# Threshold attention followed by hash routing on one core: routing in small pieces, scatters into two tables, and a leaner start

## The chip, the cores and the metric

The kernel runs on one core of one Trainium2 chip. The metric is device time in microseconds of one execution, as the median of several runs. A core has a matrix engine (TensorE, "PE" in the profile, with its weight loads shown as "PEld"), a vector engine (VectorE, "DVE"), an activation engine (ScalarE, "ACT"), a general engine (GpSimd, "POOL") and a queue engine (SyncE, "SP") that mainly issues DMA transfers. Every engine works through its own list of instructions in order and waits at semaphores for the others. In the profile "POOLq" and "SPq" are the instruction queues of these engines, where DMA transfers are issued.

## What is computed

The reference, cut to what matters:

```python
# attention: q, k, v are (8, 8, 576, 64), float32
scores = 0.125 * q @ k^T
thresh = max(scores, axis=-1) - tau
scores = where(scores >= thresh, scores, -1e9)
attn   = exp(scores - max(scores)); attn = attn / (sum(attn) + 1e-9)
out    = attn @ v
# bridge: (B, H, S, D) -> x of shape (4608, 512)
# routing: one of 8 experts per token, by its id
expert = token_ids * 2654435761 % 8
for e in range(8):
    xe = x[expert == e]
    out[expert == e] = relu(xe @ w1[e]) @ w2[e]     # w1 (8,512,1024), w2 (8,1024,512)
```

The routing depends on the token ids alone. It can therefore be worked out at any time before the first tokens are gathered for the first expert.

## The kernel before

The attention goes over 32 pairs of heads, `p` = 0 to 31, each in five steps `s` = 0 to 4 (`n = 5 p + s`): first the last 64 queries of both heads together, then four times 128 queries of each head. In each step PE computes scores, DVE turns them into `ns` (the negated scores, with their minimum accumulated), ACT takes the exponential, POOL computes the threshold `thr`, DVE masks and sums, PE transposes the weights, ACT copies them out of PSUM, and PE multiplies by v. POOL also scales the keys once per pair (`scale_k`) and adds an epsilon to the sums (`rec`). The instruction order of all engines is fixed by the program's order ("manual schedule").

The routing ranks each token within its expert, turns the rank into a slot, and writes the token's number to that slot of a table in DRAM by 36 indirect DMA transfers ("scatters") of 128 tokens each. The table is then loaded as `gidx`, by which the tokens are gathered for the experts from pair 26 on.

The loads of a pair, and the start of the kernel:

```python
def load_pair(p):
    ...
    for r in range(2):
        half = slice(64 * r, 64 * r + 64)
        nc.sync.dma_start(out=k_sb[half, 0], in_=kT[b, h0, :, S2 * r:S2 * r + S2])
        c0 = 64 * (1 - r)
        nc.sync.dma_start(out=k_sb[half, 1, c0:S2], in_=kT[b, h0 + 1, :, ...])
    nc.sync.dma_start(out=k_sb[0:64, 1, 0:64], in_=kT[b, h0 + 1, :, TAIL:S])
    for r in range(2):
        nc.sync.dma_start(out=q_sb[64 * r:64 * r + 64],
                          in_=qT[b, h0:h0 + 2].rearrange("h d s -> d h s"))

# first instructions
nc.sync.dma_start(out=tau_in[:], ...)
nc.sync.dma_start(out=tid32[:], ...)          # token ids
load_pair(0); load_v(0); load_pair(1)
make_identity(nc, ident[:])
...                                            # POOL: iotas, triangular matrix, ones, tables' fill
nc.sync.dma_start(out=slot_dram..., in_=none[:])
for w in w_bufs:                               # four buffers of 128 x 1152
    nc.vector.memset(w[:], 0.0)
...
nc.vector.memset(xg_bufs[0][:], 0.0)
for xg in xg_bufs[1:]:                         # nine copies
    nc.scalar.copy(xg[:], xg_bufs[0][:])
nc.vector.tensor_copy(iota_f[:], iota_i[:])
nc.vector.tensor_scalar(out=keep_any[:], in0=tau_in[:], ...)   # used by scale_k
```

The routing is a generator, `route()`, whose `yield` marks where a piece ends. One piece is issued ahead of the first score, and one in each step after that:

```python
def route():
    ...                                        # POOL: three memsets
    # piece 1: expert of each token, one-hot, scan along the tokens, counts by two matmuls
    nc.vector.tensor_scalar(out=eid[:], ...); nc.vector.tensor_copy(eidf[:], eid[:])
    nc.vector.tensor_tensor(out=onehot[:], ...)
    nc.vector.tensor_tensor_scan(incl[:]..., keep[:]..., onehot[:]..., ...)
    nc.vector.tensor_copy(row[:], incl[:, :, NTC - 1])
    nc.tensor.matmul(tr[:, 0, 0:E], lhsT=u128[:], rhs=row[:], start=True, stop=True)
    nc.tensor.matmul(tr[:, 0, E:2 * E], lhsT=ones128[:], rhs=row[:], start=True, stop=True)
    nc.vector.tensor_copy(cnt[:], tr[:, 0, 0:2 * E])
    ...
    yield
    ...                                        # pieces 2 to 4: base, rank, slot_i
    for c in range(NTC):                       # 36 scatters, one in each step
        yield
        ...                                    # in c = 1, 2, 3: overflow table on DVE
        nc.gpsimd.indirect_dma_start(
            out=slot_dram[:, :],
            out_offset=bass.IndirectOffsetOnAxis(ap=slot_i[:, c:c + 1], axis=0),
            in_=tok[:, c:c + 1], in_offset=None, ...)
    for _ in range(3):
        yield
    nc.sync.dma_start(out=gidx[0:TM], in_=slot_dram[0:E * CAP]...)
```

The main loop, cut to the order of what matters:

```python
for _ in range(24):
    nc.tensor.transpose(tr[:, 0, 0:P], ident[:], ident[:])    # PE works on nothing of use
next(pieces)
scale_k(0)
score(0, 0)
for n in range(LAST + NS + 1):
    p, s = divmod(n, NS)
    m = n - 2
    if s == 0: load_pair(p + 2); load_v(p + 1)
    if s == 1: scale_k(p + 1)                  # POOL
    q = p - 1
    if s == 1: add_eps(q)                      # POOL: rec
    if s == 2: nc.vector.reciprocal(recs[q][:], recs[q][:])
    ...
    negate(n, 0); expo(n, 0)                   # DVE ns, POOL thr; ACT
    if s == 0: put_xm(p - 2)                   # DVE xm, after ACT's xt
    ...
    score(n + 1, 0); negate(n, 1); expo(n, 1); score(n + 1, 1)
    ...
    for j in range(heads(n - 1)): mask(n - 1, j)               # DVE
    next(pieces, None)                         # a piece of the routing
    ...
```

Of the kernel before, what the change touches and what calls it, by code (L numbers as in the profile page):

```python
# [12 lines left out]
I32 = mybir.dt.int32  # L13
AF = mybir.ActivationFunctionType
ALU = mybir.AluOpType
AX = mybir.AxisListType
# [4 lines left out]
def kernel(  # L21
# [12 lines left out]
    nc = tc.nc  # L34

    B, H, D, S = qT.shape
    N, DIN = out.shape
    E, _, F = w1.shape
    P = 128
# [4 lines left out]
    NTC = N // P  # L44
    SCALE = 1.0 / float(D) ** 0.5
    assert D == 64 and S == 4 * P + 64 and SCALE == 0.125 and E == 8
    S2 = S // 2
    NQ = 4
    TAIL = NQ * P
# [6 lines left out]
    KT, TM = 5, 122  # L56
    CAP = KT * TM
    CH = CAP // 2
    NOV = 32
    NSLOT = -(-(E * CAP + NOV * P) // P) * P  # L60
    BIG = 1 << 20
# [4 lines left out]
    slot_dram = nc.dram_tensor("slot_scratch", (NSLOT, 1), I32, kind="Internal").ap()  # L66
# [21 lines left out]
    gidx = consts.tile([P, E, KT], I32, name="gidx")  # L88
    ov_i = consts.tile([P, NOV + 1], I32, name="ov_i")
# [28 lines left out]
    with tc.tile_pool(name="a_q", bufs=1) as a_q, \  # L118
# [29 lines left out]
        def load_pair(p):  # L148
            hp, b = divmod(p, B)
            h0 = 2 * hp  # L150
            q_sb = q_bufs[p % 3]
            k_sb = a_k.tile([P, 2, S2], FP32, name="k_sb")
            kts[p] = k_sb
            for r in range(2):
                half = slice(64 * r, 64 * r + 64)
                nc.sync.dma_start(out=k_sb[half, 0], in_=kT[b, h0, :, S2 * r:S2 * r + S2])
                c0 = 64 * (1 - r)
                nc.sync.dma_start(out=k_sb[half, 1, c0:S2],
                                  in_=kT[b, h0 + 1, :, (S2 - 64) * r:(S2 - 64) * r + S2 - c0])
            nc.sync.dma_start(out=k_sb[0:64, 1, 0:64], in_=kT[b, h0 + 1, :, TAIL:S])  # L160
            for r in range(2):
                nc.sync.dma_start(out=q_sb[64 * r:64 * r + 64],
                                  in_=qT[b, h0:h0 + 2].rearrange("h d s -> d h s"))
# [11 lines left out]
        def scale_k(p):  # L175
            nc.gpsimd.tensor_scalar(out=kts[p][:], in0=kts[p][:], scalar1=keep_any[:],
                                    scalar2=SCALE, op0=ALU.mult, op1=ALU.mult)
# [39 lines left out]
        def expo(n, j):  # L217
            c0 = 64 if n % NS == 0 else S * j
            w = w_bufs[n % NW][:, c0:c0 + S]
            ws[n, j] = w  # L220
            nc.scalar.activation(w, nss[n, j][:], AF.Exp, bias=stats[n][0][:, j:j + 1],  # L221
                                 scale=-1.0)
# [107 lines left out]
        def route():  # L330
# [24 lines left out]
            nc.gpsimd.memset(ones_e[:], 1.0)  # L355

# [4 lines left out]
            nc.vector.tensor_copy(eidf[:], eid[:])  # L361
            nc.vector.tensor_tensor(out=onehot[:],
# [3 lines left out]
            nc.vector.tensor_tensor_scan(incl[:].rearrange("p e c -> p (e c)"),  # L366
                                         keep[:].rearrange("p e c -> p (e c)"),
                                         onehot[:].rearrange("p e c -> p (e c)"),
                                         0.0, op0=ALU.mult, op1=ALU.add)
# [7 lines left out]
            nc.vector.tensor_copy(cnt[:], tr[:, 0, 0:2 * E])  # L377

# [4 lines left out]
                                    op0=ALU.logical_shift_right)  # L383
            nc.vector.tensor_copy(ot[:], ot_i[:])
            nc.vector.tensor_tensor_scan(oend[:], ones_e[:], ot[:], 0.0, op0=ALU.mult,
                                         op1=ALU.add)
            yield


            nc.vector.tensor_tensor(out=base[:], in0=oend[:], in1=ot[:], op=ALU.subtract)  # L390
            nc.vector.scalar_tensor_tensor(out=base[:], in0=base[:], scalar=8192.0,
                                           in1=cnt[:, 0:E], op0=ALU.mult, op1=ALU.add)
            nc.vector.tensor_tensor(out=incl[:], in0=incl[:],
                                    in1=base[:, :, None].to_broadcast([P, E, NTC]), op=ALU.add)
            nc.vector.tensor_tensor(out=incl[:], in0=incl[:], in1=onehot[:], op=ALU.mult)
            nc.vector.reduce_sum(rank_f[:], incl[:].rearrange("p e c -> p c e"), axis=AX.X)
            yield
            nc.vector.tensor_copy(rank_i[:, 0], rank_f[:])
            nc.vector.tensor_scalar(out=rank_i[:, 1], in0=rank_i[:, 0], scalar1=8191,
                                    scalar2=None, op0=ALU.bitwise_and)  # L400
            nc.vector.tensor_scalar(out=rank_i[:, 2], in0=rank_i[:, 0], scalar1=13, scalar2=None,
                                    op0=ALU.logical_shift_right)
            nc.vector.tensor_copy(rank[:], rank_i[:, 1])
            nc.vector.tensor_copy(ovt[:], rank_i[:, 2])
            yield
            nc.vector.tensor_scalar(out=first[:], in0=eidf[:], scalar1=float(CAP), scalar2=None,
                                    op0=ALU.mult)
            nc.vector.tensor_scalar(out=ovt[:], in0=ovt[:], scalar1=float(P),
                                    scalar2=float((E - 1) * CAP), op0=ALU.mult, op1=ALU.add)
            nc.vector.tensor_tensor(out=ovt[:], in0=ovt[:], in1=first[:], op=ALU.subtract)  # L410
            nc.vector.scalar_tensor_tensor(out=ovt[:], in0=rank[:], scalar=float(CAP),
                                           in1=ovt[:], op0=ALU.is_gt, op1=ALU.mult)
            nc.vector.tensor_tensor(out=first[:], in0=first[:], in1=rank[:], op=ALU.add)
            nc.vector.scalar_tensor_tensor(out=slot_i[:], in0=first[:], scalar=-1.0, in1=ovt[:],
                                           op0=ALU.add, op1=ALU.add)
            for c in range(NTC):
                yield
                if c == 1:
                    nc.vector.tensor_tensor(
                        out=oc[:], in0=iota_f[:, 0:NOV, None].to_broadcast([P, NOV, E]),  # L420
                        in1=oend[:, None, :].to_broadcast([P, NOV, E]), op=ALU.is_ge)
                if c == 2:
                    nc.vector.reduce_sum(ovf[:, 0:NOV], oc[:], axis=AX.X)
                if c == 3:
                    nc.vector.tensor_scalar(out=ovf[:, 0:NOV], in0=ovf[:, 0:NOV],
                                            scalar1=float(E - 1), scalar2=None, op0=ALU.min)
                    nc.vector.tensor_copy(ovf[:, NOV:NOV + 1], oend[:, E - 1:E])
                    nc.vector.tensor_copy(ov_i[:], ovf[:])
                nc.gpsimd.indirect_dma_start(
                    out=slot_dram[:, :],  # L430
                    out_offset=bass.IndirectOffsetOnAxis(ap=slot_i[:, c:c + 1], axis=0),
                    in_=tok[:, c:c + 1], in_offset=None, bounds_check=NSLOT - 1,
                    oob_is_err=False)
            for _ in range(3):
                yield
            nc.sync.dma_start(out=gidx[0:TM], in_=slot_dram[0:E * CAP].rearrange(
                "(e p k) o -> p e (k o)", e=E, k=KT))

        nc.sync.dma_start(out=tau_in[:],
                          in_=bass.AP(tensor=tau.tensor, offset=0, ap=[[0, P], [1, 1]]))  # L440
        nc.sync.dma_start(out=tid32[:],
# [3 lines left out]
        load_pair(0)  # L445
# [3 lines left out]
        nc.gpsimd.iota(iota_i[:], pattern=[[1, NOV]], base=0, channel_multiplier=0)  # L449
        make_upper_triangular(nc, u128[:], val=1.0, diag=False)  # L450
        nc.gpsimd.memset(ones128[:], 1.0)
        nc.gpsimd.memset(none[:], BIG)
        nc.gpsimd.memset(gidx[:], BIG)
        nc.gpsimd.iota(tok[:], pattern=[[1, NTC]], base=0, channel_multiplier=NTC)
        nc.sync.dma_start(out=slot_dram.rearrange("(p c) o -> p (c o)", p=P), in_=none[:])
        for w in w_bufs:
            nc.vector.memset(w[:], 0.0)
        for v_sb in v_bufs:
            nc.vector.memset(v_sb[0:64, 4, 64:P], 0.0)
            nc.vector.memset(v_sb[64:P, 4, 0:64], 0.0)  # L460
        nc.vector.memset(oT[:, 0:64], 0.0)
        nc.vector.memset(xg_bufs[0][:], 0.0)
        for xg in xg_bufs[1:]:
            nc.scalar.copy(xg[:], xg_bufs[0][:])
        nc.vector.tensor_copy(iota_f[:], iota_i[:])
# [7 lines left out]
        nc.vector.tensor_tensor(out=drop[:], in0=drop[:], in1=tau_in[:], op=ALU.max)  # L473

# [44 lines left out]
        LAST = NS * NP  # L519
        G0 = NS * ((HP - 1) * B + 2)  # L520
        pieces = route()
# [6 lines left out]
        with tc.manual_schedule():  # L528

            tr = ps_tr.tile([P, 2, 512], FP32, name="tr")  # L530
            for _ in range(24):
                nc.tensor.transpose(tr[:, 0, 0:P], ident[:], ident[:])
            next(pieces)
            scale_k(0)
            score(0, 0)
            for n in range(LAST + NS + 1):
# [12 lines left out]

                q = p - 1  # L550
# [35 lines left out]
                if n < LAST and s not in (1, 2):  # L586
                    negate(n, 0)
                    expo(n, 0)
                if s == 0 and p >= 2 and n != LAST:
                    put_xm(p - 2)  # L590
# [19 lines left out]
                next(pieces, None)  # L610
# [15 lines left out]
    with tc.tile_pool(name="m_x", bufs=1) as m_x, \  # L626
# [66 lines left out]
        with tc.For_i(0, n_ov, 1) as it:  # L693
# [11 lines left out]
            nc.gpsimd.dma_start(out=idx[:], in_=slot_dram[bass.ds(it * P + E * CAP, P), :])  # L705
# [39 lines left out]
```

## Time and profile before

| | |
|---|---|
| Time before, median of 3 runs | 1064.89 us (1064.26 to 1071.09) |
| Span of the profiled run | 1062.5 us |
| Mean granted TensorE clock | 0.987 of full speed |
| PE busy | 1023.6 us (96%) |
| DVE busy | 513.3 us (48%) |
| ACT busy | 466.8 us (44%) |
| POOL busy | 295.8 us (28%) |

How to read it: the busy shares are averages over two very different stages, the attention (until about 490 us) and the experts (after it). The profile can also be cut into windows, which give the busy time of each engine in one stretch with the granted TensorE clock; it can be shown as a timeline, in which a bracket such as [3.28 <-DVE row L370] says how long the engine stood idle ahead of the instruction and what released it; and it sums up who waited for whom. L with a number is a line of the kernel before. An instruction that is issued once per pair, such as the reciprocal, serves as a clock of the attention's progress.

### The profile page before, as it was taken

Reading aid. Unit: us, or ns where it says so; the run is one execution under the profiler, and the core shown is the slowest. Engines: PE = TensorE matmul, PEld = TensorE weight load, DVE = VectorE, ACT = ScalarE, POOL = GpSimd, SP = SyncE. Lnnn points to the kernel's source line nnn. Section 1 sums busy time; section 2 is a strip of 40 time slices with the busy share of each in tenths; the row PEclk is TensorE's granted clock in tenths of the full one; section 3 lists DMA queues with packets and bytes.
Section 4 is the critical chain, followed back from the end, with each engine's and each line's share of the span. In section 5 each row is a group of like instructions: output and inputs, shape, how many; then the busy total and the mean of one; then the engine's idle time right before and its main releaser. Section 6 shows DMA issues by size and latency. Waiting matters only on the chain. (4 is left out here: it accounts for less than half of the span.)

```text
span 1062.5 us, 20027 instructions
## 1 busy us (share of the span) xinstructions
PE 1023.6 (96%) x7438; PEld 622.7 (59%) x7438; DVE 513.3 (48%) x1347; ACT 466.8 (44%) x798; POOL 295.8 (28%) x397
## 2 busy tenths in 40 slices
PE   6989999999999999999999999999999999999996
PEld 4546566666666666665646647557465474664752
DVE  8879899999999999995410100101001001011000
ACT  5778889889889888885110000000000010000000
POOL 3555533223322226421614014031140131001001
PEclk7999999999999999999999999999999999999998
DMA  5424443444436668510234204231242132300000
GB/s 129 99 65 105 108 99 88 109 107 114 113 94 178 180 182 241 133 35 20 59 121 139 81 37 135 97 119 45 89 141 89 45 116 96 104 0 36 9 18 28
DMA packets 88292, 101.06 MB, mean 95 GB/s; under 512 B 22011, under 2 KB 63101, under 8 KB 88194
## 3 DMA queue, kind: packets, MB, share of 16 engines
q1 hardware_dynamic: 80002, 80.86, 27.3%
q0 software_dynamic: 8192, 18.91, 5.3%
q8 instruction: 60, 0.98, 0.4%
q14 instruction: 38, 0.31, 0.1%
HBM read 81.85 MB, written 19.98 MB: 96 GB/s over the span
## 5 line engine op out<-in xcount | busy, mean ns | idle before, releaser
L664 PE MATMUL o_ps<-w_sb,h 128*122 128x512 f32 x640 | 280.6, 592 | 0.0
L221 ACT ACTIVATE w<-ns,nmx 128x576 f32<-128x576 f32 x288 | 220.4, 777 | 39.8 <-DVE ns L207 39.1
L650 PE MATMUL sc<-xT,w_sb 128*128 128x305 f32 x896 | 231.2, 419 | 0.0
L232 DVE SCALAR_TENSOR_TENSOR w<-ns,thr,w 128x576 f32<-128x576 f32 x288 | 226.7, 820 | 0.5 <-POOL thr L214 0.5
L207 DVE TENSOR_SCALAR_CACHE_REDUCE ns<-sc 128x576 f32<-128x576 f32 x288 | 205.7, 747 | 9.1 <-PE sc L196 7.8
L650 PEld LDWEIGHTS sc<-xT,w_sb 128*128 128x128 f32 x896 | 169.1, 189 | 63.4 <-issue 3.4
L664 PEld LDWEIGHTS o_ps<-w_sb,h 128*122 128x122 f32 x640 | 115.6, 185 | 138.9 <-issue 138.5
L196 PE MATMUL sc<-k_sb,q 64*128 64x288 f32 (+1 forms) x1280 | 182.5, 431 | 8.1 <-DVE ns L207 8.0
L243 PEld LDWEIGHTS tr<-ident,w 64*128 64x128 f32 x2624 | 109.2, 140 | 102.3 <-ACT wT_a L264 39.1
L214 POOL TENSOR_SCALAR thr<-nmx,drop 128x2 f32<-128x2 f32 (+1 forms) x160 | 97.2, 608 | 212.0 <-DVE ns L207 205.6
L668 POOL DMA_INDIRECT out_dram<-o,gidx x40 | 39.8, 994 | 414.9 <-ACT o L667 401.3
L243 PE MATMUL tr<-ident,w 64*128 64x64 f32 x2624 | 140.2, 232 | 14.0 <-ACT wT_a L264 12.9
L667 ACT COPY o<-o_ps 122x512 f32<-122x512 f32 x40 | 23.4, 586 | 293.4 <-PE o_ps L664 293.4
L658 DVE TENSOR_SCALAR h<-sc 128x610 f32<-128x610 f32 x28 | 22.2, 794 | 256.9 <-PE sc L650 256.9
L196 PEld LDWEIGHTS sc<-k_sb,q 64*128 64x128 f32 (+1 forms) x1280 | 96.6, 181 | 28.9 <-DVE ns L207 13.1
L643 DVE COPY xT<-xT_ps 128x488 f32<-128x488 f32 x35 | 23.3, 665 | 183.4 <-PE xT_ps L641 183.4
L274 PE MATMUL av<-wT_a,v 128*64 128x320 f32 (+1 forms) x704 | 100.4, 418 | 0.8 <-DVE xm L321 0.8
L656 ACT ACTIVATE h<-sc 128x610 f32<-128x610 f32 x28 | 19.1, 680 | 182.7 <-PE sc L650 182.7
L264 ACT COPY wT_a<-tr 128x512 f32<-128x512 f32 (+1 forms) x128 | 81.8, 639 | 21.9 <-PE tr L243 21.9
L264 ACT COPY wT_b<-tr 128x512 f32<-128x512 f32 (+1 forms) x128 | 81.3, 635 | 10.8 <-PE tr L243 6.5
L274 PE MATMUL av<-wT_b,v 128*64 128x256 f32 x640 | 84.4, 394 | 0.0
L274 PEld LDWEIGHTS av<-wT_a,v 128*64 128x64 f32 x704 | 43.9, 136 | 29.2 <-DVE xm L321 1.0
(96 smaller groups left out, 527.2 us busy)
## 6 DMA issues: line engine op xcount, KB each, us to landing
w_sb<-in_moe_w_dram SPq DMA_DIRECT2D x16, 2048.0 KB
q<-in_q_dram SPq DMA_DIRECT2D x64, 288.0 KB
v<-in_v_dram SPq DMA_DIRECT2D x32, 256.0 KB
k_sb<-in_k_dram SPq DMA_DIRECT2D x96, 72.0 KB
xa_scratch<-xm SPq DMA_DIRECT2D x24, 256.0 KB
xb_scratch<-xm SPq DMA_DIRECT2D x8, 256.0 KB
k_sb<-in_k_dram SPq DMA_DIRECT2D x32, 56.0 KB
v<-in_v_dram SPq DMA_DIRECT2D x64, 16.0 KB
```

The source lines that it names most:

```text
L196: nc.tensor.matmul(sc[out_rows, i, 0:S2], lhsT=q_sb[rows, h, q0:q1], rhs=k_sb[rows, h], start=True, stop=True)
L207: nc.vector.tensor_scalar(out=ns[:].rearrange("p (i s) -> p i s", i=2), in0=sc[:, :, 0:S2], scalar1=-1.0, scalar2=None, op0=ALU.mult, op1= ...
L214: nc.gpsimd.tensor_scalar(out=thr[:, 0:j + 1], in0=stats[n][0][:, 0:j + 1], scalar1=drop[:], scalar2=None, op0=ALU.add)
L221: nc.scalar.activation(w, nss[n, j][:], AF.Exp, bias=stats[n][0][:, j:j + 1], scale=-1.0)
L232: nc.vector.scalar_tensor_tensor(out=w, in0=nss.pop((n, j))[:], scalar=stats[n][1][:, j:j + 1], in1=w, op0=ALU.is_le, op1=ALU.mult, accum_ ...
L243: nc.tensor.transpose(dst[:, r, 64 * c:64 * c + 64], src[rows, c0:c0 + P], ident[rows, rows])
L264: nc.scalar.copy(dst, tr[:, :, 0:64 * n_c].rearrange("p r (c q) -> p r c q", c=n_c))
L274: nc.tensor.matmul(av[64 * j:64 * j + 64, g, c0:c1], lhsT=v_sb[:, c, 64 * j:64 * j + 64], rhs=wT[g][:, i, c0:c1], start=(c == 0), stop=stop)
L650: nc.tensor.matmul(h_ps[:, i, 0:width], lhsT=w1_sb[:, co, fo * P:fo * P + P], rhs=xT[:, co, i * width:i * width + width], start=(co == 0), ...
L664: nc.tensor.matmul(o_ps[0:rows], lhsT=h_sb[:, fo, kt * rows:kt * rows + rows], rhs=w2_sb[:, fo, :], start=(fo == 0), stop=(fo == FO - 1))
L667: nc.scalar.copy(o_sb[0:rows], o_ps[0:rows])
L668: nc.gpsimd.indirect_dma_start(out=out[:, :], out_offset=bass.IndirectOffsetOnAxis(ap=idx, axis=0), in_=o_sb[:], in_offset=None, bounds_ch ...
```

## The change

The change has four parts.

- The routing on DVE is cut into many small pieces. They are issued in two places of a pair, ahead of the first `ns` of step 3 and ahead of `xm` of step 0, over some 14 pairs, instead of one per step at the beginning.
- The scatters have a generator of their own. It runs after the slots are known, in every step except `s == 1`, and writes even and odd columns into two tables. Both are loaded, and DVE takes the minimum of the two.
- The first loads: the keys of a pair come in three transfers instead of five, q of the first pair is issued on ACT's queue, and the token ids come after the first pair's keys and q.
- Less is cleared at first: only the margins of the four weight buffers; the clears of the gather buffers become DMA copies in pairs 3 to 11; the threshold's constants come first on DVE; POOL's constants come after the first scaling of keys. The transposes ahead of the first score are 18 instead of 24.

The diff, cut to its core:

```diff
-    slot_dram = nc.dram_tensor("slot_scratch", (NSLOT, 1), I32, kind="Internal").ap()
+    slot_dram = [nc.dram_tensor(f"slot_scratch_{i}", (NSLOT, 1), I32, kind="Internal").ap()
+                 for i in range(2)]
 ...
-        def load_pair(p):
+        def load_pair(p, q_engine=nc.sync):
 ...
+            nc.sync.dma_start(out=k_sb[0:64, :, 64:S2], in_=keys(64, -64, S2 - 64))
+            nc.sync.dma_start(out=k_sb[0:64, :, 0:64], in_=keys(0, TAIL, 64))
+            nc.sync.dma_start(out=k_sb[64:P], in_=keys(S2, -64, S2))
             for r in range(2):
-                (four transfers of keys, one of the tail, q on nc.sync)
+                q_engine.dma_start(out=q_sb[64 * r:64 * r + 64], ...)
 ...   route(): the same operations, with 31 yields between them; the scan in two halves
-            for c in range(NTC):
-                yield
 ...
+        def scatters():
+            for c in range(NTC):
                 nc.gpsimd.indirect_dma_start(
-                    out=slot_dram[:, :],
+                    out=slot_dram[c % 2][:, :],
 ...
+                yield
+            for _ in range(4):
+                yield
+            for table, dst in zip(slot_dram, (gidx, gidx_odd)):
+                nc.sync.dma_start(out=dst[0:TM], in_=table[0:E * CAP]...)
+            for _ in range(4):
+                yield
+            nc.vector.tensor_tensor(out=gidx[:], in0=gidx[:], in1=gidx_odd[:], op=ALU.min)
 ...
         nc.sync.dma_start(out=tau_in[:], ...)
+        load_pair(0, nc.scalar)
         nc.sync.dma_start(out=tid32[:], ...)
-        load_pair(0)
 ...   keep_any and drop now ahead of the clears
         for w in w_bufs:
-            nc.vector.memset(w[:], 0.0)
+            nc.vector.memset(w[:, 0:64], 0.0)
+            nc.vector.memset(w[:, 64 + S:P + S], 0.0)
 ...
-        for xg in xg_bufs[1:]:
-            nc.scalar.copy(xg[:], xg_bufs[0][:])
 ...
-            for _ in range(24):
+            for _ in range(18):
                 nc.tensor.transpose(tr[:, 0, 0:P], ident[:], ident[:])
+            scale_k(0)
+            constants()
             next(pieces)
-            scale_k(0)
             score(0, 0)
 ...
+                if s == 3 and n < LAST:
+                    next(pieces, None)
+                if s == 1 and 3 <= p < 2 + len(xg_bufs):
+                    nc.sync.dma_start(out=xg_bufs[p - 2][:], in_=xg_bufs[0][:])
 ...
+                if s == 0 and n < LAST:
+                    next(pieces, None)
                 if s == 0 and p >= 2 and n != LAST:
                     put_xm(p - 2)
 ...
-                next(pieces, None)
+                if s != 1 and placed:
+                    next(scatter_pieces, None)
```

## The prediction

> **What bounds the kernel now.** I began with the summary and the 40 slices: TensorE (PE) is busy 96% of the span, and only the first slice falls well short. The span is therefore TensorE's own work plus a few holes, so the change can only fill holes. After about 500 us PE is at 100% and at full clock, and the change doesn't touch that part. I look at the first 150 us.
>
> Next, the windows of the start (columns: window, length, busy us and count of PE, weight loads, DVE, ACT, POOL; then granted clock, DMA share, GB/s):
>
> ```profile
> 1.60:6.85 5.25, 5.24 (x24) 4.98 (x24) 4.36 (x11) 0.58 (x1) 1.19 (x9) 1.00 0.37 73
> 6.85:10.13 3.28, 0.00 (x1) 0.03 (x1) 2.90 (x11) 2.65 (x6) 0.75 (x1) 0.98 1.05 251
> ...
> 16.00:31.00 15.00, 13.16 (x108) 8.46 (x106) 14.52 (x50) 9.72 (x16) 6.28 (x7) 0.54 0.49 121
> 31.00:35.60 4.60, 4.60 (x54) 2.77 (x52) 1.79 (x9) 3.10 (x5) 2.04 (x3) 1.00 0.45 94
> ```
>
> PE does its 24 idle transposes, stands still for 3.28 us, and then works at about half clock until 31 us. The timeline of that start (start, duration, engine, line, operation) shows why it stands still:
>
> ```profile
> 4.99 1.30 SPq L162 DMA_DIRECT2D q<-in_q_dram  x2
> ...
> 7.37 0.10 DVE L469 TENSOR_SCALAR keep_any<-tau_in 128x1 f32<-128x1 f32 x1
> ...
> 7.58 0.75 POOL L176 TENSOR_SCALAR k_sb<-k_sb,keep_any 128x576 f32<-128x576 f32 x1 [4.73 <-DVE eid L359]
> ...
> 10.13 0.17 PE L374 MATMUL tr<-row,u 128*128 128x8 bf16 x1 [3.28 <-DVE row L370]
> ...
> 10.26 3.49 PE L196 MATMUL sc<-k_sb,q 64*64 64x288 f32 x16
> ```
>
> The scores need q, issued last at 4.99, and scaled keys, which need `keep_any`, behind the long memsets on DVE. Then they sit behind the routing's matmul L374, which waits for DVE's `row`. First score: 10.26.
>
> For the rhythm I read the once-per-pair reciprocal on DVE:
>
> ```profile
> 35.65 0.22 DVE L554 RECIPROCAL rec<-rec 128x9 f32<-128x9 f32 x1 [2.82 <-POOL rec L302]
> 50.00 0.21 DVE L554 RECIPROCAL rec<-rec 128x9 f32<-128x9 f32 x1 [0.15 <-POOL rec L302]
> 69.06 0.22 DVE L554 RECIPROCAL rec<-rec 128x9 f32<-128x9 f32 x1 [4.67 <-POOL rec L302]
> 84.50 0.20 DVE L554 RECIPROCAL rec<-rec 128x9 f32<-128x9 f32 x1
> 100.27 0.22 DVE L554 RECIPROCAL rec<-rec 128x9 f32<-128x9 f32 x1 [1.35 <-POOL rec L302]
> 116.83 0.22 DVE L554 RECIPROCAL rec<-rec 128x9 f32<-128x9 f32 x1 [2.54 <-POOL rec L302]
> 131.22 0.22 DVE L554 RECIPROCAL rec<-rec 128x9 f32<-128x9 f32 x1
> ```
>
> Later pairs come every 14.40 us (203.13, 217.53, 231.93). Here the gaps are 14.35, **19.06, 15.44, 15.77, 16.56**, 14.39: the four long ones hold 4.66+1.04+1.37+2.16 = 9.2 us. The scatters explain them, as the timeline of the longest shows:
>
> ```profile
> 62.16 1.02 POOL L429 DMA_INDIRECT slot_scratch<-tok,slot_i  x1 [1.62 <-DMA slot_scratch<-tok,slot_i]
> ...
> 66.83 1.05 POOL L429 DMA_INDIRECT slot_scratch<-tok,slot_i  x1 [3.31 <-DMA slot_scratch<-tok,slot_i]
> 67.92 0.76 POOL L176 TENSOR_SCALAR k_sb<-k_sb,keep_any 128x576 f32<-128x576 f32 x1
> 68.76 0.26 POOL L302 TENSOR_SCALAR rec<-rs 128x9 f32<-128x9 f32 x1
> ```
>
> Each scatter writes the same table and waits until the one before has landed. At a pair's beginning the loads of q, k and v slow that landing; POOL stands 3.3 us, key scaling and `rec` queue behind it, then DVE (4.67 us) and PE (3.5 us).
>
> What slack do steady pairs have? The waits of DVE between 145 and 450 us (total, times, longest):
>
> ```profile
> DVE xm L321 <- ACT xt L312: 8.8, 21, 0.4
> DVE ns L207 <- PE sc L196: 5.2, 21, 0.4
> ```
>
> So DVE waits 0.42 + 0.25 = 0.67 us per pair (8.8/21, 5.2/21). PE is busy 14.03 of 14.40 us in such a pair.
>
> **What the skill says.** "DMA: Bandwidth & Descriptors", section "Anatomy of one DMA", gives about 2.0 us fixed cost per DMA, mostly the write's receipt. The trace agrees: scatters land 2.2/2.5/4.4 us after issue (min/median/max). Its section "Issuing engines are not separate DMA queues" says that a second issuer saves only issue time: q on ACT's queue saves its place in SP's line, no bandwidth. The trace of before has one such issuer and can't show it. "TensorE: Matmul & The Clock Gate", "Part 1", says that an idle window of about 3.4 us halves the clock. The trace agrees in kind: after the 3.28 us hole the clock was 0.54 (16 to 31 us), after the 3.5 us hole at 66 it was 0.66 from 70 to 75.
>
> **The change, part by part.**
>
> *Start, up to the first score.* SP now issues tau (0.91 to 1.32) and three key transfers at 0.6 us each, done by about 3.2; q goes out on ACT at about 1 to 2.3, perhaps after its 1.28 us table load. q and keys together are 576 KB. At 190 to 250 GB/s (5 to 10 us in before showed 184, the hole 251) that is 2.3 to 3 us; with landing time I put the keys at 5.5 to 6.0. `keep_any` is first on DVE and ready near 3.3. Key scaling (0.75) ends near 6.5, and no routing matmul stands ahead: **first score at 6.6**, 3.7 us earlier. The 18 transposes end at 1.6 + 18 x 0.218 = 5.5, leaving a PE hole of 1.1 us instead of 3.28, so I expect the clock to stay near 1.0. DVE's remaining clears (about 14 of 0.1 to 0.17, one of 0.48) end by about 6.8, before its first `ns` at 7.6 (first score plus 1.0; 1.53 in before at low clock).
>
> *From the first `ns` to the first reciprocal.* In before: 11.79 to 35.65 = 23.86 us. DVE's attention work in it is 12 `ns` steps of 0.68 and 10 masks of 0.74 (start to start) = 15.6. Routing took 2.37+0.61+0.97+0.41+0.33+0.42 = 5.1 (gaps between the attention steps), and DVE waited 2.82 for POOL and 0.34 for PE: total 23.9, so it closes. After: 15.6, plus 0.8 for the eid, cast and one-hot that stay here, plus 1.0 for fill and PE: 17.4. First reciprocal at 7.6 + 17.4 = 25.0, **10.6 us earlier**, which includes the 3.7. A check from PE: at the steady rhythm a reciprocal comes 6.2 us after its pair's first score, hence 6.6 + 14.4 + 6.2 = 27.2 if the first pair already took 14.4; it has no products to do, so 25 is possible and 27 the cautious value.
>
> *Scatters.* They start at pair 12 (slot_i is in the 26th piece, two per pair), four per pair for nine pairs, alternating tables. Each then waits for the second before it, issued at least two steps (5.7 us) earlier, above the longest landing of 4.4. POOL has room: steady pairs use 4.2 of 14.4 us, scatters add 4 x 1.04. In before the pair from 116.83 to 131.22 held five scatters and took 14.39. So the 9.2 us go, and nothing comes back here: **-9.2**.
>
> *Routing in pieces.* About 6.5 us of DVE work is spread over pairs 1 to 14, into 0.67 x 14 = 9.4 us of waits. Large pieces (scans 0.4, add 0.46, multiply 0.88, reduce 0.64) stand ahead of `xm`, where 0.42 is free; 0.05 to 0.5 each spills. Small ones of 0.2 ahead of the fourth step delay expo and a transpose slightly. The two count matmuls make DVE and PE wait for each other once, about 0.7. Together **+2**.
>
> *The rest.* Nine ACT copies (4.77 us) become SBUF copies by DMA in pairs 3 to 11; ACT wasn't the bound there, so 0. The final minimum (one small DVE operation) and the second table's load: +0.1. The clearing of a second table is hidden.
>
> Sum: 1064.9 - 10.6 - 9.2 + 2.1 = 1047.2. Since the start's check leans later, I say **1048**.
>
> **Rivals.** (1) *DVE becomes the bound*: at 95% busy (13.7 of 14.4), each piece costs its full length. For: PE's only wait in a steady pair is behind ACT and DVE. Against: the pieces stand where DVE waits. It would cost 6.5 instead of 2: 1052. (2) *PE at half clock binds the first pair*: early steps load PE only about 60%, and at half clock it needs about 20 us for that pair. Start gain falls to 5 or 6: 1052. (3) *Scatters still cost*, because POOL's queue is in order and each takes 1.04 even without a wait; half of the 9.2 returns: 1052. Two together give 1056. (4) Everything absorbed and the first reciprocal at 23.2: 1044.
>
> **Range and chances.** The holes to be filled are 10.6 + 9.2, perhaps 1.8 more at the start: the floor is 1043.3, while 2% is 1043.6. So over 2% faster is nearly out of reach. One rival gives 1052, one and a half 1054. Range 1044 to 1054; faster 0.06, within 2% 0.93, slower 0.01.
>
> **What would show it.** First score near 6.6 with no clock below 0.9 from 6 to 30; first reciprocal near 25; gaps of 14.4 to 14.6 in pairs 1 to 14 (rival 1: 14.9); no POOL wait on slot_scratch; scatter pairs at 14.4 (rival 3: above 14.8); everything from pair 25 on merely shifted. The prediction fails if q on ACT lands late, or if a piece's delay travels through DVE, ACT and PE and isn't recovered in its pair.

## The result, and the profile after

The changed kernel takes 1055.51 us (median of 4 runs, 1054.17 to 1055.59) against 1066.76 us for the kernel before in the same session (1064.26 to 1071.09); the ratio is 0.9887 with a 95% interval of 0.985 to 0.9925. So it is faster by about 1.1%, but 7.5 us slower than predicted and outside the predicted range. The span of the profiled run fell from 1062.5 to 1053.8 us.

First the timeline of the start of the changed kernel (start, duration, engine, line, operation; in brackets the idle time ahead and its releaser):

```profile
0.90 1.36 ACTq L167 DMA_DIRECT2D q<-in_q_dram  x2
...
2.81 0.61 SPq L165 DMA_DIRECT2D k_sb<-in_k_dram  x1
...
8.65 0.75 POOL L181 TENSOR_SCALAR k_sb<-k_sb,keep_any 128x576 f32<-128x576 f32 x1 [7.17 <-DMA k_sb<-in_k_dram]
...
9.45 5.06 PE L201 MATMUL sc<-k_sb,q 64*64 64x288 f32 x24 [3.82 <-POOL k_sb L181]
...
10.83 0.76 DVE L212 TENSOR_SCALAR_CACHE_REDUCE ns<-sc 128x576 f32<-128x576 f32 x1 [6.19 <-PE sc L201]
```

The keys' three transfers are all issued by 3.4 us, yet POOL waits for them until 8.65. The first score is at 9.45, only 0.8 us earlier than before (10.26); the PE hole ahead of it is 3.82 us, longer than the old one of 3.28.

Next the clock of progress, the reciprocal of each pair on DVE, at the start and around pair 12, where the scatters begin:

```profile
27.97 0.20 DVE L605 RECIPROCAL rec<-rec 128x9 f32<-128x9 f32 x1
43.69 0.21 DVE L605 RECIPROCAL rec<-rec 128x9 f32<-128x9 f32 x1
58.37 0.20 DVE L605 RECIPROCAL rec<-rec 128x9 f32<-128x9 f32 x1
73.30 0.21 DVE L605 RECIPROCAL rec<-rec 128x9 f32<-128x9 f32 x1
87.72 0.21 DVE L605 RECIPROCAL rec<-rec 128x9 f32<-128x9 f32 x1
...
174.46 0.21 DVE L605 RECIPROCAL rec<-rec 128x9 f32<-128x9 f32 x1
189.38 0.20 DVE L605 RECIPROCAL rec<-rec 128x9 f32<-128x9 f32 x1
204.42 0.20 DVE L605 RECIPROCAL rec<-rec 128x9 f32<-128x9 f32 x1
219.46 0.20 DVE L605 RECIPROCAL rec<-rec 128x9 f32<-128x9 f32 x1
```

The four long gaps of before are gone. In their place are a first gap of 15.72 and, from 174.46 on, gaps of 14.92 and then 15.04 for all nine scatter pairs; the rhythm between is 14.43. Adding up the gaps between reciprocals in both traces gives a full account (us; gap g is between the reciprocals of pairs g-1 and g, counting pairs from 0):

| Stretch | before | after | difference |
|---|---|---|---|
| start to first reciprocal | 35.65 | 27.97 | -7.68 |
| gap 1 | 14.35 | 15.72 | +1.37 |
| gaps 2 to 5 (the long gaps of before) | 66.83 | 58.46 | -8.37 |
| gaps 6 to 10 | 71.90 | 72.31 | +0.41 |
| gaps 11 to 19 (scatters of after) | 129.76 | 135.22 | +5.46 |
| gaps 20 to 31 | 172.97 | 172.88 | -0.09 |
| sum, to the last reciprocal | 491.46 | 482.56 | -8.90 |

What is a scatter pair's extra 0.6 us? The page of after has one group on DVE that grew. Here it is, in before and in after, and then the timeline around step 0 of one scatter pair:

```profile
L232 DVE SCALAR_TENSOR_TENSOR w<-ns,thr,w 128x576 f32<-128x576 f32 x288 | 226.7, 820 | 0.5 <-POOL thr L214 0.5
```

```profile
L237 DVE SCALAR_TENSOR_TENSOR w<-ns,thr,w 128x576 f32<-128x576 f32 x288 | 232.0, 838 | 0.0
```

```profile
230.02 1.04 POOL L466 DMA_INDIRECT slot_scratch<-tok,slot_i  x1 [0.40 <-issue]
230.23 0.81 DVE L237 SCALAR_TENSOR_TENSOR w<-ns,thr,w 128x576 f32<-128x576 f32 x1
...
230.97 1.50 DVE L237 SCALAR_TENSOR_TENSOR w<-ns,thr,w 128x576 f32<-128x576 f32 x1
...
231.10 0.76 POOL L181 TENSOR_SCALAR k_sb<-k_sb,keep_any 128x576 f32<-128x576 f32 x1
```

The masks take 232.0 us in all, 5.3 more than the 226.7 of before, which is nearly the 5.46 of the table. One mask per scatter pair takes 1.50 us (the first of them 1.30) instead of 0.81. It isn't the one that runs beside the scatter (0.81 at 230.23), but the one beside the key scaling, which the scatter has pushed from its old place, beside `xm`, into the masks. The excess of 0.69 us is nearly the whole length of the scaling (0.76), as if the two ran one after the other. The mask reads two operands from SBUF. "GPSIMD Engine Reference", section "1. Specifications", says that GpSimd's SBUF interfaces are shared with VectorE, with contention in instructions with two SBUF inputs; this trace agrees, with 1.50 against 0.81. That was my theory for the experiments: a collision of scaling and mask, brought about by the scatter of step 0.

For the start the theory was that q, on its own queue, goes ahead of the keys. The queue table for two windows of after (queue: packets, MB, share of the 16 DMA engines' time, which can overlap and pass 100%; q10 is ACT's queue with q alone, q1 is SP's, with the keys and what is issued behind them), first from 4 to 5 us, then from 6 to 7 us:

```profile
q10 hardware_dynamic: 114, 0.23, 71.5%
q1 hardware_dynamic: 113, 0.09, 35.2%
```

```profile
q1 hardware_dynamic: 323, 0.18, 100.2%
q10 hardware_dynamic: 22, 0.03, 15.0%
```

q has most of the engines until it is nearly through, and only then do the keys get them.

### The profile page after: what moved, and what is told of

It is laid out like the page before. It is cut to its first block, busy times and chain, and to the rows that moved or that the text cites. A ratio compares the mean times of both kernels' runs of the same rounds, so it can differ in the third digit from the quotient of the medians.

```text
span 1053.8 us, 19892 instructions
## 1 busy us (share of the span) xinstructions
PE 1020.7 (97%) x7432; PEld 618.5 (59%) x7432; DVE 513.1 (49%) x1352; ACT 462.5 (44%) x789; POOL 306.0 (29%) x399
## 5 line engine op out<-in xcount | busy, mean ns | idle before, releaser
L237 DVE SCALAR_TENSOR_TENSOR w<-ns,thr,w 128x576 f32<-128x576 f32 x288 | 232.0, 838 | 0.0
L219 POOL TENSOR_SCALAR thr<-nmx,drop 128x2 f32<-128x2 f32 (+1 forms) x160 | 102.2, 639 | 223.5 <-DVE ns L212 213.1
```

The costliest lines, as they stand in the source:

```text
L219: nc.gpsimd.tensor_scalar(out=thr[:, 0:j + 1], in0=stats[n][0][:, 0:j + 1], scalar1=drop[:], scalar2=None, op0=ALU.add)
L237: nc.vector.scalar_tensor_tensor(out=w, in0=nss.pop((n, j))[:], scalar=stats[n][1][:, j:j + 1], in1=w, op0=ALU.is_le, op1=ALU.mult, accum_ ...
```

## The experiments

They ran on several chips. The stretch after the last reciprocal is 571 to 573 us on one of them, for the kernels before and after alike, and 582 to 584 us on the others, so times are only set against runs of the same chip (as ratios to the kernel before), and the attention's gaps are compared directly.

### Scatters out of step 0

```diff
-                if s != 1 and placed:
+                if s != 0 and placed:
```

> The scatters leave out step 0 instead of step 1, so none stands in POOL's list ahead of the key scaling; their number and tables stay. Theory (the step-0 scatter pushes the key scaling of 0.75 us into the time of a mask, and DVE and POOL, both on two SBUF operands or long ones, hold each other up): the gaps between reciprocals of the nine scatter pairs fall from 15.04 to 14.4 to 14.5, DVE's masks lose the long ones of 1.50 us, the time falls by 5 to 6 us to about 1050. Rival (each scatter costs POOL and DVE about 0.15 us wherever it stands): the gaps stay at 15.0 and the time at 1055.

Measured: gaps 11 to 19 add up to 132.42 us instead of 135.22, and no mask in them is longer than 0.87 us. The last reciprocal came at 480.42. The ratio to before is 0.9864 (0.981 to 0.9918), which can't be told from the changed kernel's 0.9887; only the gaps can. The scaling now runs beside `xm`, and both masks behind it keep their length:

```profile
228.79 0.74 POOL L181 TENSOR_SCALAR k_sb<-k_sb,keep_any 128x576 f32<-128x576 f32 x1
229.15 0.69 DVE L326 TENSOR_TENSOR xm<-av,rec 128x512 f32<-128x512 f32 x1 [0.54 <-ACT xt L317]
229.76 0.81 DVE L237 SCALAR_TENSOR_TENSOR w<-ns,thr,w 128x576 f32<-128x576 f32 x1
...
230.49 0.81 DVE L237 SCALAR_TENSOR_TENSOR w<-ns,thr,w 128x576 f32<-128x576 f32 x1
```

The long masks went, as the theory says, but only half the time came back: eight of the gaps stayed at 14.67 to 14.99. On another chip the same placement gave 14.43 in every scatter pair (the last experiment but one), so the rest isn't the placement's alone; what it is on this chip was not settled. In five of these pairs PE stands still for 0.35 us ahead of a transpose with no releaser shown, which the traces from the chip with 571 to 573 us don't show there; but the next experiment, on the same chip, has this hole in all nine pairs and still runs seven of them in 14.4.

### The scaling left out in the scatter pairs

```diff
-                if s == 1 and p + 1 < NP:
+                if s == 1 and p + 1 < NP and not 12 <= p <= 21:
                     scale_k(p + 1)
```

The keys of these pairs stay unscaled, so this kernel computes something else; its time is read for the gaps alone.

> The scatters stay as in the changed kernel, but the key scaling is left out in pairs 12 to 21 (the keys of these pairs stay unscaled, so the output differs). Theory (the collision is between the key scaling and the mask): the gaps of the scatter pairs fall to 14.4 to 14.5 although every scatter is still there, no mask over 1.0 us in them. Rival (the scatter itself delays the thresholds or the mask): the gaps stay at about 15.0.

Measured: every scatter stands where the change has it, and gaps 11 to 19 add up to 130.47 us: seven are 14.39 to 14.44, the other two 14.76 and 14.77. No long mask is left. So the scatter alone costs next to nothing (0.6 us over nine pairs against the 129.87 of nine gaps of 14.43); it is the scaling beside the mask that cost 4.75 of the 5.35. That it isn't just POOL's missing work is shown by the last two experiments, which keep every scaling.

### One table in the changed kernel

```diff
-                    out=slot_dram[c % 2][:, :],
+                    out=slot_dram[0][:, :],
```

> All scatters of the changed kernel go into the first table; the second stays as filled and the minimum is still taken, so the output is unchanged. If the second table is what removed the stalls of 9.2 us: scatters wait for the landing of the one before (4.3 us median in the changed kernel against steps of 2.9 us), POOL idles on slot_scratch for 1 to 3 us many times, gaps of the scatter pairs rise to 15.5 to 17, time 5 to 15 us above the changed kernel. Rival (leaving out one step and the later place did it): gaps stay near 15.0.

Measured: gaps 11 to 19 are 14.92 to 17.28 and add up to 147.71 us, 12.5 more than with two tables; the ratio to before is 1.0002 (0.9986 to 1.0019). POOL's timeline has the old picture again: the scatter of step 0 waits (the releaser is put down to a load of v, but with two tables the same scatter doesn't wait), with scaling, `rec` and the threshold behind it.

```profile
197.99 0.33 POOL L219 TENSOR_SCALAR thr<-nmx,drop 128x1 f32<-128x1 f32 x1
202.68 1.14 POOL L466 DMA_INDIRECT slot_scratch<-tok,slot_i  x1 [4.37 <-DMA v<-in_v_dram]
203.87 0.76 POOL L181 TENSOR_SCALAR k_sb<-k_sb,keep_any 128x576 f32<-128x576 f32 x1
204.71 0.26 POOL L307 TENSOR_SCALAR rec<-rs 128x9 f32<-128x9 f32 x1
```

Without the second table the whole change would have brought nothing.

### Two tables alone in the kernel before

```diff
-                    out=slot_dram[:, :],
+                    out=slot_dram[c % 2][:, :],
     (and the second table's clearing, loading and minimum)
```

> The kernel before with one part of the change alone: scatters alternate between two tables, still one in every step from step 3 on. If the waits for landing made the four long gaps, they lose most of their 9.2 us, and the collision of scatter, scaling and mask costs up to 0.6 in each of seven pairs: 4 to 9 us faster than before, about 1058. Rival (early place of the scatters, beside the routing on DVE and a slow clock, made them): less than 3 us.

Measured: ratio 0.9941 (0.9921 to 0.996). The first reciprocal came at 32.72 instead of 35.65, and gaps 1 to 6 were 16.80, 15.81, 15.60, 15.59, 15.61 and 15.97. They add up to 95.38 us; before has 95.57. The waits for landing are gone (no scatter waits longer than 0.43 us), yet nothing of the six gaps has come back. The time fell by 4.3 us, the low end of what I had expected, but in another place: 2.9 us of it came ahead of the first reciprocal, if this chip's kernel before starts like the one traced on the other chip (35.65; it was 35.03 when traced once more). The timeline shows what took the place of the waits:

```profile
91.57 1.04 POOL L431 DMA_INDIRECT slot_scratch<-tok,slot_i  x1 [0.42 <-DMA k_sb<-in_k_dram]
91.71 0.69 DVE L323 TENSOR_TENSOR xm<-av,rec 128x512 f32<-128x512 f32 x1 [1.03 <-ACT xt L314]
92.32 0.97 DVE L234 SCALAR_TENSOR_TENSOR w<-ns,thr,w 128x576 f32<-128x576 f32 x1
92.65 1.24 POOL L178 TENSOR_SCALAR k_sb<-k_sb,keep_any 128x576 f32<-128x576 f32 x1
93.21 0.08 DVE L234 DVE_READ_ACCUMULATOR w<-ns,thr,w 128x1 f32 x1
93.21 1.28 DVE L234 SCALAR_TENSOR_TENSOR w<-ns,thr,w 128x576 f32<-128x576 f32 x1
```

Here the scaling lies across two masks: it takes 1.24 us instead of 0.75, the masks 0.97 and 1.28. The six gaps are 8.8 us above the rhythm of 14.43. The twelve long masks hold 4.3 of them, and `xm` waits 0.71 to 1.06 us for ACT's `xt` in these pairs instead of 0.41 behind them, which is another 3.2; why ACT comes later was not tested. So about half of what replaced the waits is the collision, and in the kernel before the waits had mostly kept it away.

### The start: q behind the keys on SP

```diff
-        load_pair(0, nc.scalar)
+        load_pair(0)
```

> The first pair's q goes out on SP's queue behind its keys instead of on ACT's. Theory (q on a second queue, in rows of 2304 bytes, takes about 70% of the DMA engines from 4 to 6 us and keeps the keys, in rows of 256 to 1152 bytes, back): key scaling starts at 5.5 to 6.5 instead of 8.65, then q is the last to land, first score at 7.5 to 8.5 instead of 9.45. Rival (the keys' small rows are slow by themselves): scaling still at 8 or later, first score at 9.5 or later.

Measured, in the timeline of this kernel's start:

```profile
5.87 0.75 POOL L181 TENSOR_SCALAR k_sb<-k_sb,keep_any 128x576 f32<-128x576 f32 x1 [4.40 <-DMA k_sb<-in_k_dram]
7.48 1.19 PE L201 MATMUL sc<-k_sb,q 64*64 64x288 f32 x2 [1.86 <-DMA q<-in_q_dram]
8.89 4.69 PE L201 MATMUL sc<-k_sb,q 64*64 64x288 f32 x18 [0.22 <-DMA q<-in_q_dram]
```

The keys are there at 5.87, inside the 5.5 to 6.0 of the prediction and 2.8 us earlier than in the changed kernel: their small rows aren't slow by themselves. Now q is last, its second half at 8.89. The first reciprocal comes at 27.42 and the ratio is 0.9846 (0.9805 to 0.9887). The ratios of this and the next two experiments can't be told from the changed kernel's; the times of the start can be.

### The start: keys on both queues

```diff
-            nc.sync.dma_start(out=k_sb[64:P], in_=keys(S2, -64, S2))
+            q_engine.dma_start(out=k_sb[64:P], in_=keys(S2, -64, S2))
             for r in range(2):
-                q_engine.dma_start(
+                (q_engine, nc.sync)[r].dma_start(
```

> The third transfer of the first pair's keys goes out on ACT's queue ahead of one half of q, the other half of q on SP's queue behind the keys. Theory (keys kept back by q): scaling at about 6, first score at 7 to 8, a PE hole under 2.5 us, clock at 1.0 from 8 to 20, the time 2 to 4 us below the changed kernel. Rival (the bytes of everything in flight set the start, in whatever order): first score at 9 or later, no gain.

Measured: scaling at 6.88, first score at 7.69, first reciprocal at 26.28, 1.7 us earlier than in the changed kernel. The clock didn't stay up: 0.84 from 5 to 10 us, 0.82 from 10 to 15 and 0.71 from 20 to 25, and the first gap was 15.87. The ratio is 0.9856 (0.9811 to 0.99).

### The start: v and the second pair held back

```diff
-        load_v(0)
-        load_pair(1)
 ...
             scale_k(0)
+            nc.gpsimd.memset(v_bufs[0][:, 0, 0:1], 0.0)
+            load_v(0)
+            load_pair(1)
             constants()
```

> q stays on ACT's queue; the first v and the second pair's q and keys are held back until the first key scaling is done, by a one-column clear of v on POOL ahead of them. Theory (q is what keeps the keys back): the scaling moves little, 8.0 to 8.7. Rival (v and the token ids, issued behind the keys, share their queue's bandwidth): the scaling moves to 6.5 to 7.5 and the first score to 7.3 to 8.3.

Measured: scaling at 8.37, first score at 9.17, 0.28 us better than the changed kernel; ratio 0.9863 (0.9822 to 0.9904). So v and the second pair, issued behind the keys, hardly hold them back (the token ids stayed where they were); q does.

These three runs also show what the collision costs when it is larger. Two, four and four of their scatter pairs took 15.51 to 15.80 us, and in exactly these pairs the scaling lies across two masks: it takes 1.24 to 1.25 us, and both masks are long (1.12 and 1.29 us in one of these pairs, 0.89 and 1.28 in another). In the other scatter pairs, mostly at 15.03 to 15.06, one mask is long. With the keys on both queues the early start was lost again, in these pairs (2.0 us) and in the pairs behind them (1.2 us): the last reciprocal came at 484.19, against 482.56 in the changed kernel.

### The changed kernel and the kernel before once more

> The changed kernel once more, on the chip of the runs sent with it, so that they can be set against it. First reciprocal at 28, gaps of 15.0 in pairs 12 to 20; the ratio to before 0.985 to 0.993. The first gap after the start is 15.7 if TensorE's clock falls after the 3.9 us hole, 14.35 if it stays (both were seen with the same start).

> The kernel before, with a trace, on the same chip. Gaps as in the first trace (19.1, 15.4, 15.8, 16.6 in pairs 1 to 5). If this chip lands DMA later than the first one, the hole between attention and experts is longer here in before as well as in the changed kernel, and the difference of the times of the two chips lies there alone.

Measured on one chip: the changed kernel 1054.35 us, ratio 0.9872 (0.9831 to 0.9913), with the same gaps of 15.03 to 15.04, but a **first gap of 14.34** instead of 15.72; the kernel before with gaps 18.64, 15.83, 16.69 and 16.35, and 572.7 us from its last reciprocal to the end. From 20 to 30 us the granted clock (third number from the end) was 0.79 and 0.87 in the first run of the changed kernel:

```profile
20.00:25.00 5.00, 3.50 (x40) 2.50 (x42) 5.00 (x16) 3.66 (x7) 1.93 (x3) 0.79 0.52 135
25.00:30.00 5.00, 5.00 (x54) 3.16 (x54) 4.04 (x12) 2.84 (x6) 1.32 (x3) 0.87 0.54 106
```

In the run repeated here it was 1.00 in both windows:

```profile
20.00:25.00 5.00, 3.33 (x52) 2.32 (x52) 5.00 (x16) 3.88 (x7) 1.76 (x3) 1.00 0.47 124
25.00:30.00 5.00, 5.00 (x56) 2.78 (x54) 5.00 (x14) 3.92 (x8) 1.68 (x4) 1.00 0.56 117
```

In the ten traces of the changed kernel and its variants the first gap goes with the clock of this stretch: 14.34 to 14.36 in the six with 1.00 in both windows, 14.67 with 0.80 and 1.00, and 15.72 to 15.87 in the three that were below 1.00 in both. It doesn't go with the clock right behind the hole: from 10 to 15 us that was 0.53 in the run without scalings and 0.50 in the run of the last experiment, and their first gaps were 14.36 and 14.35. The first scores came at 9.45 and 9.50. So the 1.37 us of gap 1 in the first table belong to the run and its clock, and not to the change.

### Scatters in steps 1 to 4, keys on both queues, 26 transposes

This joins the edits of the first and the fifth experiment, and lengthens the idle transposes:

```diff
-            for _ in range(18):
+            for _ in range(26):
```

> Keys on both queues, scatters in steps 1 to 4, and 26 transposes instead of 18, so that TensorE has no hole ahead of the first score. Theory: first score at 7.7, clock at 1.0 from 5 to 35, first reciprocal at 26 and the gap after it 14.4 instead of 15.7, scatter pairs 14.4 to 14.8: 4 to 6 us below the changed kernel on the same chip. Rival (the clock falls later anyway, while the first steps load TensorE only in part): the gap after the first reciprocal stays above 15.3.

Measured: **1047.68 us**, ratio 0.98 (0.976 to 0.9841), against 1054.35 of the changed kernel on the same chip. First score at 7.59, clock 1.00 in all windows from 5 to 35 us, first gap 14.36. The reciprocals at the start and in the scatter pairs:

```profile
25.47 0.20 DVE L605 RECIPROCAL rec<-rec 128x9 f32<-128x9 f32 x1
39.83 0.21 DVE L605 RECIPROCAL rec<-rec 128x9 f32<-128x9 f32 x1
...
185.01 0.21 DVE L605 RECIPROCAL rec<-rec 128x9 f32<-128x9 f32 x1
199.44 0.21 DVE L605 RECIPROCAL rec<-rec 128x9 f32<-128x9 f32 x1
213.87 0.21 DVE L605 RECIPROCAL rec<-rec 128x9 f32<-128x9 f32 x1
```

All scatter pairs take 14.42 to 14.43, as pairs without scatters do. The transposes can't be credited with the steady clock, since the run just before had it with the hole left in.

### Scatters in steps 2 to 4 only

```diff
-                if s != 1 and placed:
+                if s > 1 and placed:
     (one pause instead of four ahead of the tables' load, three instead of four behind it)
```

> Scatters in steps 2, 3 and 4 only, three per pair over twelve pairs, with shorter pauses ahead of and behind the load of the tables. If the 0.28 us per pair that were left with scatters in steps 1 to 4 come from the scatter of step 1: gaps of 14.43 in pairs 12 to 23, 5 to 6 us below the changed kernel. If any scatter costs a little: 14.6 to 14.7 over twelve pairs, 3 us below it.

Measured: gaps of 14.42 to 14.43 in all twelve scatter pairs, 1049.17 us, ratio 0.9819 (0.9779 to 0.9859), 5.2 us below the changed kernel on the same chip. That is the 5.46 of the table, brought back by a place for the scatters that isn't ahead of the scaling. As the experiment before it gives 14.43 with step 1 in use too, a scatter in step 1 isn't by itself what kept the first experiment at 14.7.

## Why the prediction was wrong

**Where it held.** The removal of the long gaps and the cost of the pieces were put at -9.2 and +2, together -7.2; gaps 2 to 10 measure -8.37 + 0.41 = -7.96. From the first `ns` to the first reciprocal I had 17.4 us; it was 27.97 - 10.83 = 17.14. The count matmuls' mutual wait was put at 0.7; the gap that holds it is 14.93, 0.50 over the rhythm. Nothing moved from pair 20 on (-0.09).

**The first step that failed: "first score at 6.6".** It rested on the keys' landing at 5.5 to 6.0, from the bytes of q and keys at the bandwidth of before. Both the bytes and the order were wrong. I had counted 576 KB for q and keys together. q alone is that much, two transfers of 288 KB, as the page of after lists them (the keys' third transfer, of 32 KB, is not among its lines):

```profile
q<-in_q_dram SPq DMA_DIRECT2D x62, 288.0 KB
k_sb<-in_k_dram SPq DMA_DIRECT2D x32, 144.0 KB
k_sb<-in_k_dram SPq DMA_DIRECT2D x32, 112.0 KB
```

The sum is 864 KB, and at my 190 to 250 GB/s that is an estimated 3.5 to 4.7 us instead of 2.3 to 3. As for the order, q on ACT's queue took 71.5% of the DMA engines' time from 4 to 5 us, and the keys came after it, at 8.65. I had cited that a second issuing engine gives no bandwidth of its own, and still treated the second queue as saving "its place in SP's line" without asking whose place it takes. The keys are needed first, because their scaling comes ahead of the score. The size of the error is 9.45 - 6.6 = 2.85 us, and the first reciprocal missed by 27.97 - 25.0 = 2.97. The experiment with q behind the keys shows who held the keys back: they come at 5.87 there, but q not before 8.89. With the keys at the head of both queues the first score came at 7.59 and 7.69, so the order is worth about 1.8 of the 2.85 us. Some 1.0 is left in the best order tried; the 288 KB that I missed (1.2 to 1.6 us by the same estimate) would explain it, but no run moved fewer bytes, so this part is argued. The PE hole I expected at 1.1 us became 3.82, and the clock I expected at 1.0 fell in that run; with the same start it stayed up in another, so a further 1.37 us of the miss, in gap 1, is not the change's.

**The second: "nothing comes back here".** I counted POOL's room (4.2 of 14.4 us busy) and the absence of waits, both correct: POOL waited for no table in after. What I left out is that an instruction on POOL can lengthen one on DVE without any semaphore between them. The rival "scatters still cost" gave the right outcome and nearly the size (half of 9.2 against 5.46), but by a wrong mechanism: it blamed POOL's queue, and with the scaling left out the scatters in the same places cost 0.6 us over nine pairs.

My evidence that scatters are free, a pair of before with five scatters in 14.39 us, was misread. In before the scatter of step 0 often waited so long that the scaling fell past the masks, in that very pair too:

```profile
127.92 0.81 DVE L232 SCALAR_TENSOR_TENSOR w<-ns,thr,w 128x576 f32<-128x576 f32 x1
128.23 1.42 POOL L429 DMA_INDIRECT slot_scratch<-tok,slot_i  x1 [1.25 <-DMA slot_scratch<-tok,slot_i]
129.69 0.76 POOL L176 TENSOR_SCALAR k_sb<-k_sb,keep_any 128x576 f32<-128x576 f32 x1
130.01 1.05 DVE L232 SCALAR_TENSOR_TENSOR w<-ns,thr,w 128x576 f32<-128x576 f32 x1
```

Only four masks of its first 150 us are longer than 0.87 us. The kernel before with two tables and almost no such wait has two long masks in every one of these pairs, and gaps 1.2 to 2.4 us over the rhythm (the long masks add 0.6 to 1.0 us of it). The 9.2 us were therefore not to be had by taking the wait away. The changed kernel got them because its scatters left these pairs altogether, and it paid 5.46 us where they went.

Together: 1047.2 (the prediction's sum) + 2.97 (start) + 1.37 (clock of that run) + 5.46 (collision) - 0.76 (gaps 2 to 10: 7.96 against 7.2) = 1056.2, against the measured 1055.5. The kernel with both faults mended ran at 1047.68, where the prediction had put the change. That the number agrees so well is in part luck: its first score was 1.0 us later than predicted, and its gaps 2 to 10 saved 0.8 us more.

What stays open is why the first experiment kept about 0.3 us per scatter pair on its chip, why `xt` came later in the kernel before with two tables, and what decides when the clock falls.

## What to carry to other kernels

Ahead of moving work onto an engine with room, look at what it pushes back in that engine's list, and at what runs on the neighbour at the new time: a wait removed can uncover a collision that the wait had hidden. When loads go to a second queue, add up the bytes of every transfer and put what is needed first at the head of both queues. A once-per-iteration instruction, listed with its start times, accounts for a change to a tenth of a microsecond where the busy shares show nothing.

## What the runs showed of the hardware that I had not expected

- A long element-wise instruction on POOL and a two-operand one on DVE can hold each other up: the mask took 1.50 instead of 0.81 us beside the scaling, which then kept its 0.76, and the scaling took 1.24 instead of 0.75 beside two masks. `xm`, which reads one large operand from PSUM, kept its 0.69 us beside the scaling, and a scatter on POOL left the mask at 0.81.
- Two DMA queues didn't share evenly here: q's queue, with rows of 2304 bytes, had about twice the engines' time of SP's (71.5% against 35.2%), with the keys in rows of 256 to 1152 bytes, although the keys' first transfer was issued only half a microsecond later. That the length of the rows is the reason was not tested.
- After holes of about the same length with the same start (3.82, 3.87 and 4.01 us), the clock from 10 to 15 us was 0.74, 1.00 and 0.50 in three runs. So a hole longer than the 3.4 us that the prediction cites didn't always lower it. In the first of these runs it was back at 1.00 from 15 to 20 us and fell again, to 0.79, behind a stretch in which PE was busy for 3.53 of 5 us. "TensorE: Matmul & The Clock Gate", "Part 1", says that the window in which activity is measured runs free of the program; the three values agree with that, and no run here tests it.
- The changed kernel's scatters, which don't wait for one another, landed later: 4.3 and 3.4 us after issue (medians of two runs), against 2.5 in both traces of before. They also run at another time of the attention, so the cause isn't shown.
